# Attention and mixture of experts on one core: matmuls without a reader in the first 28 microseconds

## The chip, the cores and the metric

One core of a Trainium2 chip runs the whole program in one launch. The metric is the device time of that core in microseconds; the time before is 882.89 us, the median of three runs (879.62, 882.89 and 883.45). The core has five engines that each work off a queue of their own in order: TensorE (PE in the profile; PEld are its weight loads), VectorE (DVE), ScalarE (ACT), GpSimd (POOL) and SyncE (SP), which here only starts transfers. [...]

## The reference

Inputs q, k, v have 8 batches, 8 heads, 576 positions and 64 dimensions, in float32. Attention comes first, on rotated q and k:

```
q_rot, k_rot = (rotate(q), rotate(k))
scores = scale * np.matmul(q_rot, k_rot.transpose(0, 1, 3, 2))
attn = softmax(scores)             # over the last axis
x = (attn @ v).transpose(0, 2, 1, 3).reshape(4608, 512)
```

Then each of the 4608 rows of x goes to one of 8 experts, the one with the largest of `x @ w_gate + modality_bias[modality_id]`, and comes out as `gate * (relu(x @ w1[e]) @ w2[e])`, with w1 of 512 x 1024 and w2 of 1024 x 512.

## The kernel before

The attention is worked in 32 pairs of heads (n = 0 to 31), and the experts follow from about 460 us on. A pair passes through these steps, each a Python function that issues instructions:

- `load` brings q and k of the pair, transposed, into a buffer (ST in the profile); `rope_` rotates them in five parts: two products (0 and 1, lines 454 and 456), their sum (2, line 458), a copy that rounds the sum to the matmul's input form (3, by `acopy`, line 445, on ScalarE, into HL), and the remainder of the rounding (4, line 462, also into HL). For pair 0 the vector parts run on VectorE, for pair 1 parts 0 to 2 on VectorE and part 4 on GpSimd, later all on GpSimd.
- `swap` (line 470) copies HL into SW by transfers, with the two halves of 64 partitions exchanged, first the rounded part, then the remainder.
- `scores` (line 485), nine times for a pair (S0 to S8): matmuls of 64 x 128 by 64 x 288, two side by side on the two halves of the rows, one from HL and one from SW, into a slot of two PSUM banks. S0 to S7 take six matmuls each, S8 twelve. There are four slots, ps0 to ps3 (`SL` in the code).
- `rowmin` (line 494, VectorE) takes a slot, writes it to SBUF with the row minimum and frees the slot; `expo` (line 503, ScalarE) takes the exponential.
- `fill` (F0 to F3, FA, FB; `tpose` at line 508) transposes the exponentials on TensorE, 16 instructions of 64 columns in F0 to F3, four in FA, into a slot; `evac` copies the slot out, one bank by ScalarE and one by VectorE (lines 445 and 541).
- `AV` (line 566) multiplies by v; `outp` and `ev` finish the pair.

Pair 0 is rotated in three pieces of columns, `FIRST = ((0, 480), (800, 1152), (480, 800))`, so that the first piece can start early. idf, an identity matrix of 128 x 128, is written by GpSimd at the start.

The order on every engine is fixed by hand. Each step is put into a list of jobs with a time as its key (`KEYS`, and `EDGE` for the first and last pairs, plus 14.438 us for each pair), the list is sorted, and the instructions are issued in that order; PE, ACT, DVE, POOL and SP keep it. For pair 0 TensorE's order is S8, S0, S1, S2, S3, S5, S6, S4, S7, F1, F0, F2, FA, and then the first scores of pair 1, S2, S4, S1, S8, S3, and FB and S0, before the first `AV` of pair 0. `take` chooses a slot when the job is issued, and the framework adds the semaphore waits that the buffers ask for. Pair 0's pieces are rotated by the loop at line 1427, ahead of all these jobs.

Of the kernel before, what the change touches and what calls it, by code (L numbers as in the profile page):

```python
# [53 lines left out]
SLOTS = {  # L54
    "S0": 1, "S1": 2, "S2": 3, "S3": 0, "S4": 2, "S5": 0, "S6": 2, "S7": 0, "S8": 1, "F0": 1, "F1": 3, "F2": 0, "F3": 3, "FA": 2,
    "FB": 2, "AVA": 0, "AVB": 3, "OUT": 1, "RK8": 5, "L1": 0,
}
# [173 lines left out]
def tile_attention_moe(ctx: ExitStack, tc: tile.TileContext, qk, v, mod, wg, mb, w1, w2, rope, cf, ci, out):  # L231
    nc = tc.nc
# [9 lines left out]
    idf = cst.tile([P, P], F32, name="idf")  # L242
# [19 lines left out]
    HL, SW = ([cst.tile([P, 2, TW], F32R, name=f"{nm}{i}") for i in range(2)] for nm in ("HL", "SW"))  # L262
# [45 lines left out]
    SL = [psS.tile([P, 2, 512], F32, name=f"ps{i}") for i in range(4)]  # L308
# [3 lines left out]
    def take(nm, bks, n=None):  # L312

        own = PLACES.get(n, {}).get(nm, SLOTS[nm])
        if nm == "RK8":
            own, bks = own & 3, (own >> 2,)
        if not all((own, b) in idle for b in bks):
            if nm == "RK8":
                own, b = min(idle, key=idle.get)
                bks = (b,)  # L320
            else:
                own = min((i for i in range(4) if all((i, b) in idle for b in bks)), key=lambda i: max(idle[i, b] for b in bks))
        for b in bks:
            del idle[own, b]
        if len(bks) == 2:
            use[own] = []
        return (own, *bks) if nm == "RK8" else own
# [15 lines left out]
    def load(n, half):  # L343
        nc.sync.dma_start(out=Rs[n % 2][:, half], in_=qk[n, :, half])
        st[n] = dict(R=Rs[n % 2], HL=HL[n % 2], SW=SW[n % 2], V=Vs[n % 2])
# [98 lines left out]
    def acopy(o, i, scale=1.0):  # L444
        return nc.scalar.activation(o, i, AF.Copy, scale=scale)  # L445


    def rope_(n, part, c0=0, c1=QW):
        d = st[n]
        e = nc.vector if n == 0 or n == 1 and part < 3 else nc.gpsimd  # L450
        c, o = slice(c0, c1), slice(c0 + 64, c1 + 64)
        a, b = d["R"][:, 0, c], d["R"][:, 1, c]
        if part == 0:
            e.tensor_tensor(a, a, COS[:, c], op=ALU.mult)
        elif part == 1:
            e.tensor_tensor(b, b, SIN[:, c], op=ALU.mult)
        elif part == 2:
            e.tensor_tensor(a, a, b, op=ALU.add)  # L458
        elif part == 3:
            acopy(d["HL"][:, 0, o], a)  # L460
        else:
            e.tensor_tensor(d["HL"][:, 1, o], a, d["HL"][:, 0, o].bitcast(F32), op=ALU.subtract)  # L462

    def swap(n, i, c0=0, c1=QW, eng=nc.sync):
        d = st[n]
        a, b = (d[t].bitcast(F32) for t in ("SW", "HL"))
        for g in range(2):
            c = slice(max(c0 + 64, Q0[0] * g), min(c1 + 64, TW - 64 if g else K1[1]))
            if c.start < c.stop:
                eng.dma_start(out=a[g * 64:g * 64 + 64, i, c], in_=b[64 - g * 64:128 - g * 64, i, c])  # L470
# [35 lines left out]
    def tpose(ps, g, c, src, k0):  # L506
        r = slice(g * 64, g * 64 + 64)
        nc.tensor.transpose(ps[:, g, c:c + 64], src[r, k0:k0 + P], idf[r, r])  # L508

    def fill(n, f):  # L510
        d = st[n]
        own = take(f, (0, 1), n)
        ps = SL[own]
        d[f], d["at", f] = ps, own
        if f[1] in "0123":
            j = int(f[1])
            for i in range(8):
                for g in range(2):
                    tpose(ps, g, i * 64, PJ[j], (S + 64) * (i // 4) + i % 4 * P)
        elif f == "FA":  # L520
            for j in range(2):
                for g in range(2):
                    tpose(ps, g, j * 64, PJ[j], 512)
        else:
            for kt in range(4):
                for g in range(2):
                    tpose(ps, g, kt * 64, P4, 64 + g * 64 + kt * P)
            for g in range(2):
                tpose(ps, g, 256, P4, (1 - g) * S)
            for j in (2, 3):  # L530
                for g in range(2):
                    tpose(ps, g, 192 + j * 64, PJ[j], 512)
# [891 lines left out]
    order.enter_context(tc.manual_schedule(engines=pinned))  # L1424
    dmas = ExitStack()
    dmas.enter_context(tc.manual_schedule(engines={mybir.EngineType.SP}))
    for i, c in enumerate(FIRST):
        for part in range(5):
            rope_(0, part, *c)
            if part > 2:  # L1430
                swap(0, part - 3, *c, eng=(nc.scalar, nc.sync)[part - 3])
        if i == 0:
            load(1, 0)
# [4 lines left out]
    for n in range(NPAIR):  # L1438
# [7 lines left out]
        for f in ("F0", "F1", "F2", "F3", "FA", "FB"):  # L1446
            K_(f, fill, n, f)
            for g in range(2):
                K_(f"{'AB'[g]}_{f}", evac, n, f, g)
        for w in range(2):  # L1450
            c = "AB"[w]
# [243 lines left out]
```

## Time and profile before

| | |
|---|---|
| median of three runs | 882.89 us (879.62 to 883.45) |
| profiled execution, its own time | 888.49 us |
| its span, first to last instruction | 886.6 us, mean granted clock 0.988 |
| PE busy | 838.3 us (95%) |
| DVE busy | 725.3 us (82%) |
| ACT busy | 622.3 us (70%) |
| POOL busy | 649.0 us (73%) |
| chain that ended last, by engine | PE 79%, DVE 7%, issue 5%, ACT 4%, POOL 4%, DMA 1% |

Busy time is an average over the whole span, and says little on the first 30 us. The chain that ended last is followed back from the last instruction, at each step to what released it; "issue" in it is time for which the profile shows no wait. In a timeline a line has the start, the time from first start to last end of a merged group, the engine, the line of the code, the operation, what is written from what, the shape and the number of instructions; in brackets stands the idle time before it and what ended that. Matmuls are pipelined, so the distance from one start to the next tells more than the duration of one.

### The profile page before, as it was taken

Reading aid. Unit: us, or ns where it says so; the run is one execution under the profiler, and the core shown is the slowest. Engines: PE = TensorE matmul, PEld = TensorE weight load, DVE = VectorE, ACT = ScalarE, POOL = GpSimd, SP = SyncE. Lnnn points to the kernel's source line nnn. Section 1 sums busy time; section 2 is a strip of 40 time slices with the busy share of each in tenths; the row PEclk is TensorE's granted clock in tenths of the full one; section 3 lists DMA queues with packets and bytes.
Section 4 is the critical chain, followed back from the end, with each engine's and each line's share of the span. In section 5 each row is a group of like instructions: output and inputs, shape, how many; then the busy total and the mean of one; then the engine's idle time right before and its main releaser. Section 6 shows DMA issues by size and latency. Waiting matters only on the chain.

```text
span 886.6 us, 24920 instructions
## 1 busy us (share of the span) xinstructions
PE 838.3 (95%) x9504; PEld 690.8 (78%) x9504; DVE 725.3 (82%) x1612; ACT 622.3 (70%) x1325; POOL 649.0 (73%) x507
## 2 busy tenths in 40 slices
PE   2899999999999999999989799999999998999995
PEld 2687777777777777777768689898989896989895
DVE  6788888898898988888878788989988986798562
ACT  2897989889898888887964467565646563646453
POOL 3899988988989989999358888886886865334111
PEclk9999999999999999999999999999999998999999
DMA  8766868878788786755847292244445321521330
GB/s 266 222 191 169 265 171 213 175 202 207 193 204 195 201 202 173 223 153 155 228 126 237 86 187 74 78 128 159 159 143 185 109 73 34 167 86 52 113 140 22
DMA packets 84346, 141.06 MB, mean 159 GB/s; under 512 B 27592, under 2 KB 54364, under 8 KB 83192
## 3 DMA queue, kind: packets, MB, share of 16 engines
q1 hardware_dynamic: 73624, 118.28, 49.2%
q0 software_dynamic: 9248, 19.46, 7.0%
q8 instruction: 77, 1.26, 0.6%
q10 hardware_dynamic: 1344, 1.62, 0.6%
q14 instruction: 53, 0.43, 0.2%
HBM read 104.61 MB, written 19.51 MB: 140 GB/s over the span
## 4 chain that ended last, share of the span: by engine, by line
PE 79%; DVE 7%; issue 5%; ACT 4%; POOL 4%; DMA 1%; POOLq 0%; SPq 0%; DVEq 0%; ACTq 0%
PE psY L1326 18%; PE ps L566 16%; PE ps L485 14%; PE psH L1194 12%; PE ps L508 9%; PE ps L601 3%; PE psY L1194 2%; PE ps L1079 1%; PE psH L1079 1%; PE psY L1098 1%; ACT P L503 1%; DVE X L1155 1%; POOL HL L462 1%; DVE W1L L442 1%; DMA SW<-HL 1%
## 5 line engine op out<-in xcount | busy, mean ns | idle before, releaser
L494 DVE CUSTOM_DVE_ANT_1 sc<-ps,ZERO 128x576 f32<-128x576 f32 x288 | 206.6, 749 | 24.8 <-PE ps L485 14.6
L503 ACT ACTIVATE P<-sc,mn 128x576 f32<-128x576 f32 x256 | 196.0, 769 | 5.7 <-DVE mn L494 5.1
L485 PE MATMUL ps<-HL 64*128 64x288 f32 x960 | 170.9, 312 | 14.9 <-ACT HL L445 10.7
L485 PE MATMUL ps<-SW 64*128 64x288 f32 x960 | 170.4, 313 | 5.8 <-DMA SW<-HL 5.6
L485 PEld LDWEIGHTS ps<-HL 64*128 64x128 f32 x960 | 136.5, 191 | 20.7 <-ACT HL L445 10.7
L485 PEld LDWEIGHTS ps<-SW 64*128 64x128 f32 x960 | 136.3, 191 | 10.2 <-issue 7.7
L566 PE MATMUL ps<-PH,AT 128*64 128x320 f32 (+1 forms) x1024 | 139.3, 414 | 2.1 <-DVE PH L541 1.9
L1194 PE MATMUL psH<-HL,W1H 128*128 128x256 f32 x576 | 123.3, 283 | 5.8 <-ACT TB L445 3.0
L1013 POOL DMA_INDIRECT XG<-X,iy x80 | 106.9, 1336 | 29.7 <-issue 20.7
L541 DVE COPY PH<-ps 128x512 f32<-128x512 f32 (+1 forms) x160 | 98.4, 631 | 14.3 <-PE ps L508 8.5
L445 ACT ACTIVATE PH<-ps 128x512 f32<-128x512 f32 (+1 forms) x160 | 85.3, 551 | 33.1 <-PE ps L508 23.1
L566 PEld LDWEIGHTS ps<-PH,AT 128*64 128x64 f32 x1024 | 68.3, 137 | 51.1 <-DVE PH L541 5.3
L1194 PE MATMUL psH<-HL,W1L 128*128 128x256 f32 x384 | 107.9, 281 | 0.0
L462 POOL TENSOR_TENSOR HL<-ST,HL 128x1152 fp32r<-128x1152 f32 x31 | 82.4, 2657 | 34.3 <-ACT HL L445 34.2
L508 PEld LDWEIGHTS ps<-idf,P 64*128 64x128 f32 x2304 | 86.7, 138 | 21.7 <-ACT P L503 9.2
L1326 PE MATMUL psY<-W2H,SW 128*128 128x512 f32 x256 | 102.0, 399 | 1.5 <-issue 1.5
L1013 POOL DMA_INDIRECT AT<-X,iy x68 | 88.2, 1297 | 20.4 <-issue 18.3
L1326 PE MATMUL psY<-W2L,SW 128*128 128x512 f32 x256 | 101.5, 396 | 0.7 <-issue 0.7
L508 PE MATMUL ps<-idf,P 64*128 64x64 f32 x2304 | 98.2, 225 | 3.7 <-ACT AT L445 1.6
L1194 PEld LDWEIGHTS psH<-HL,W1H 128*128 128x128 f32 x576 | 96.1, 190 | 7.1 <-ACT TB L445 3.2
L1109 POOL DMA_INDIRECT out_dram<-sc,ix x36 | 41.8, 1162 | 68.7 <-ACT sc L1108 60.6
L458 POOL TENSOR_TENSOR ST<-ST 128x1152 f32<-128x1152 f32 x30 | 79.6, 2653 | 1.2
(281 smaller groups left out, 1984.7 us busy)
## 6 DMA issues: line engine op xcount, KB each, us to landing
ST<-in_moe_w_dram SPq DMA_DIRECT2D x88, 512.0 KB
ST<-in_qk_dram SPq DMA_DIRECT2D x62, 576.0 KB
SW<-HL SPq DMA_DIRECT2D x124, 216.0 KB
AT<-in_v_dram SPq DMA_DIRECT2D x32, 256.0 KB
X<-X SPq DMA_DIRECT2D x8, 1024.0 KB
XG<-X,iy POOLq DMA_INDIRECT x80
AT<-X,iy POOLq DMA_INDIRECT x68
AT<-in_v_dram SPq DMA_DIRECT2D x64, 16.0 KB
```

The lines of the kernel that those rows point to most:

```text
L445: return nc.scalar.activation(o, i, AF.Copy, scale=scale)
L458: e.tensor_tensor(a, a, b, op=ALU.add)
L462: e.tensor_tensor(d["HL"][:, 1, o], a, d["HL"][:, 0, o].bitcast(F32), op=ALU.subtract)
L485: nc.tensor.matmul(ps[:, g, 0:288], t[:, wq, q0:q0 + P], t[:, wk, k0:k0 + 288], start=(m == 0), stop=(m == len(L) - 1))
L494: nc.vector.tensor_tensor_reduce(sc, d.pop(("S", u))[:, :, 0:288], ZERO.unsqueeze(2).to_broadcast([P, 2, 288]), 1.0, FMAX, ALU.add, ALU.mi ...
L503: nc.scalar.activation(p, sc.rearrange("p a b -> p (a b)"), AF.Exp, bias=mn, scale=-1.0, accum_out=d["sum"][:, u:u + 1])
L508: nc.tensor.transpose(ps[:, g, c:c + 64], src[r, k0:k0 + P], idf[r, r])
L541: alone(d["at", f], g, (nc.vector.tensor_copy if g else acopy)(o, i).ins, int(f[1] in "23B"))
L566: i = nc.tensor.matmul(pa[hh * 64:hh * 64 + 64, 0:c1 - c0], d["V"][:, hh, kt, :], r, start=(kt == 0), stop=(kt == 4))
L1013: inst = nc.gpsimd.indirect_dma_start(out=x[:, t, g, :], out_offset=None, in_=X.rearrange("n (i f) -> (n i) f", f=P)[0:rows], in_offset=ba ...
L1194: nc.tensor.matmul(ps[b][:, r * BLK:r * BLK + BLK], w[:, c, f0:f0 + P], x[:, c, :], start=(first and r == 0 and c == 0 and i == 0), stop=( ...
L1326: nc.tensor.matmul(po[t], hx[:, c, o:o + P], w[:, c, :], start=(k == 0 and c == 2 * q and i == 0), stop=(k == 3 and c == 2 * q + 1 and i = ...
```

## The change

The change adds matmuls whose results nothing reads. It takes nothing away and keeps the order of all other instructions. A helper `turns` issues k matmuls into bank 0 of the slot that S8 of pair 0 will use, before S8 takes it. Fourteen are issued from idf, and then, behind part 3 of the rotation of each of pair 0's three pieces, 9, 14 and 20 from the piece that the copy has just written, with 480, 352 and 320 columns. In `fill`, two matmuls of 480 columns go ahead of the transpositions of F0, F1, F2 and FA of pair 0, into the slot that these transpositions then overwrite.

```
+    def turns(k, w, x):
+        for _ in range(k):
+            nc.tensor.matmul(SL[SLOTS["S8"]][:, 0, 0:x.shape[-1]], w, x, start=True, stop=True)
+
     def fill(n, f):
         d = st[n]
         own = take(f, (0, 1), n)
         ps = SL[own]
+        if n == 0 and f in ("F0", "F1", "F2", "FA"):
+            for _ in range(2):
+                nc.tensor.matmul(ps[:, 0, 0:480], HL[0][:, 0, 64:192], HL[0][:, 0, 64:544], start=True, stop=True)
         d[f], d["at", f] = ps, own
...
+    turns(14, idf, idf)
     for i, c in enumerate(FIRST):
         for part in range(5):
             rope_(0, part, *c)
+            if part == 3:
+                turns((9, 14, 20)[i], HL[0][:, 0, 64:192], HL[0][:, 0, c[0] + 64:c[1] + 64])
             if part > 2:
                 swap(0, part - 3, *c, eng=(nc.scalar, nc.sync)[part - 3])
```

## Rows read from the trace of the kernel before

**Rows 1.** The chain of waits in order of time: start, us, what

```profile
1.67 0.28 POOL idf masks.py:199
...
20.12 2.65 POOL HL L462
...
23.30 6.11 DMA SW<-HL
...
29.46 3.98 PE ps L485 x25
...
34.38 2.38 PE ps L566 x20
```

**Rows 2.** Waits of TensorE, 30 to 60 us: us in total, times, longest

```profile
PE ps L485 <- DMA SW<-HL: 0.4, 1, 0.4
```

**Rows 3.** Timeline of ScalarE, first copies into HL

```profile
7.42 0.60 ACT L445 ACTIVATE HL<-ST 128x480 fp32r<-128x480 f32 x1 [0.70 <-DVE ST L458]
...
10.18 0.50 ACT L445 ACTIVATE HL<-ST 128x352 fp32r<-128x352 f32 x1 [2.16 <-DVE ST L458]
...
12.59 0.47 ACT L445 ACTIVATE HL<-ST 128x320 fp32r<-128x320 f32 x1 [1.92 <-DVE ST L458]
...
18.87 1.17 ACT L445 ACTIVATE HL<-ST 128x1152 fp32r<-128x1152 f32 x1 [5.80 <-DVE ST L458]
```

**Rows 4.** Timeline of VectorE, pair 1's rotation and first row minima

```profile
16.08 1.36 DVE L454 TENSOR_TENSOR ST<-ST,ST 128x1152 f32<-128x1152 f32 x1 [1.22 <-DMA ST<-in_qk_dram]
17.48 1.36 DVE L458 TENSOR_TENSOR ST<-ST 128x1152 f32<-128x1152 f32 x1
19.88 0.76 DVE L494 CUSTOM_DVE_ANT_1 sc<-ps,ZERO 128x576 f32<-128x576 f32 x1 [1.05 <-PE ps L485]
...
21.84 0.76 DVE L494 CUSTOM_DVE_ANT_1 sc<-ps,ZERO 128x576 f32<-128x576 f32 x1 [0.51 <-PE ps L485]
```

**Rows 5.** Timeline of TensorE, 16 to 30 us

```profile
16.58 0.58 PE L485 MATMUL ps<-SW 64*128 64x288 f32 x1 [5.25 <-DMA SW<-HL]
...
18.21 0.44 PE L485 MATMUL ps<-HL 64*128 64x288 f32 x1
...
18.45 0.44 PE L485 MATMUL ps<-HL 64*128 64x288 f32 x1
...
23.57 0.29 PE L485 MATMUL ps<-SW 64*128 64x288 f32 x1
23.70 0.29 PE L485 MATMUL ps<-HL 64*128 64x288 f32 x1
...
25.06 1.29 PE L508 MATMUL ps<-idf,P 64*128 64x64 f32 x32 [0.38 <-ACT P L503]
27.01 0.84 PE L508 MATMUL ps<-idf,P 64*128 64x64 f32 x20 [0.65 <-ACT PH L445]
28.60 0.37 PE L485 MATMUL ps<-HL 64*128 64x288 f32 x1 [0.76 <-ACT AT L445]
```

**Rows 6.** Stretches of TensorE: us, busy (instructions), granted clock, DMA share, GB/s

```profile
29.00:30.00 1.00, 0.64 (x6) 0.65 0.89 336
30.00:31.00 1.00, 1.00 (x12) 0.50 0.20 72
...
32.00:33.00 1.00, 1.00 (x13) 0.65 0.69 221
```

**Rows 7.** Chain of waits, a stretch of matmuls of 256 columns

```profile
465.60 12.15 PE ps L1079 x96
```

**Rows 8.** TensorE, a later gap: its timeline, then a stretch as in rows 6

```profile
448.43 0.37 PE L485 MATMUL ps<-HL 64*128 64x288 f32 x1 [2.09 <-ACT PH L445]
...
449.00:450.00 1.00, 1.00 (x14) 0.57 0.44 91
```

**Rows 9.** Timeline of GpSimd at 356 us

```profile
356.24 2.66 POOL L462 TENSOR_TENSOR HL<-ST,HL 128x1152 fp32r<-128x1152 f32 x1 [0.39 <-ACT HL L445]
```

More of the change, by code (lines that the diff above doesn't have):

```diff
@@ L508, in tpose, with turns @@
         nc.tensor.transpose(ps[:, g, c:c + 64], src[r, k0:k0 + P], idf[r, r])
+    def turns(k, w, x):
+        for _ in range(k):
+            nc.tensor.matmul(SL[SLOTS["S8"]][:, 0, 0:x.shape[-1]], w, x, start=True, stop=True)
     def fill(n, f):
@@ L513, in fill @@
         ps = SL[own]
+        if n == 0 and f in ("F0", "F1", "F2", "FA"):
+            for _ in range(2):
+                nc.tensor.matmul(ps[:, 0, 0:480], HL[0][:, 0, 64:192], HL[0][:, 0, 64:544], start=True, stop=True)
         d[f], d["at", f] = ps, own
@@ L1426, in tile_attention_moe @@
     dmas.enter_context(tc.manual_schedule(engines={mybir.EngineType.SP}))
+    turns(14, idf, idf)
     for i, c in enumerate(FIRST):
@@ L1429, in tile_attention_moe @@
             rope_(0, part, *c)
+            if part == 3:
+                turns((9, 14, 20)[i], HL[0][:, 0, 64:192], HL[0][:, 0, c[0] + 64:c[1] + 64])
             if part > 2:
```

## The prediction

> **What bounds the kernel now.** I read the page's busy shares first (TensorE 95% of the span), then the chain of waits in order of time, because a change to the first 30 us can only count through what that chain holds there. In the chain the reader is to see that TensorE is not on it before 29.46 us [rows 1]: it goes through GpSimd's subtraction for pair 1 (line 462, 20.12 to 22.77), then a transfer SW<-HL of 6.11 us that lands at 29.41, and only then through TensorE's scores of pair 1. From there on TensorE is the chain almost without a break: in the waits of 30 to 60 us it has a single one, 0.4 us, and none in 60 to 90 [rows 2].
>
> What leads to 20.12 contains no TensorE either. ScalarE's copy of pair 1 runs 18.87 to 20.04 [rows 3], after VectorE's sum of 17.48 to 18.84, after VectorE's product at 16.08, which waited for a load of q and k [rows 4]. So 29.41 is set by a load, three vector steps, one ScalarE copy, one GpSimd step and one transfer. Whatever the change gains before 29.41 is gained beside this path. It can pay in one way only: by the speed of TensorE after 29.46.
>
> That speed is the second thing to see [rows 5, 6]. Pairs of score matmuls (one per half of the rows, side by side) follow each other by 0.24 us at 18.21 and 18.45, and by 0.13 us at 23.57 and 23.70. The granted clock is recorded as 1.00 in both stretches, so the record does not show the slow start; the spacing does. [...] Between 25.06 and 29.3 TensorE had done 52 transpositions and a few scores. [...]
>
> **The change part by part.**
>
> *Fourteen matmuls of idf.* idf is written by 1.95 us [rows 1]. Nearest rows: 20 plain f32 matmuls of 256 columns took 2.38 us at full clock, 0.12 each [rows 1], so 0.06 for 128 columns, 0.12 at half clock: 14 x 0.12 = 1.7 us. No row shows a plain f32 matmul of full height and width, so I set the upper end at four times that (6.7 us, to 8.7). The lower end is 14 x 0.06 = 0.8. The next matmuls wait for ScalarE's first copy, done at 8.02 [rows 3]: at the upper end 0.7 us late, otherwise nothing. I take 1.7, by that nearest row.
>
> *Nine, fourteen and twenty matmuls of 480, 352 and 320 columns.* Nearest row: 96 matmuls of 256 columns in 12.15 us, 0.127 each at full clock [rows 7]; by columns that is 0.24, 0.17 and 0.16 us, and twice as much at half clock. They wait for copies that end at 8.02, 10.68 and 13.06 [rows 3]. All at full clock: 8.02 + 2.1 = 10.2; 10.7 + 2.4 = 13.1; 13.1 + 3.2 = 16.3, just ahead of 16.58, when the first scores get their transfer [rows 5]. All at half clock: 8.0 + 4.3 = 12.3, + 4.8 = 17.1, + 6.4 = 23.5, which would make the first scores 6.9 us late. The clock will rise between: in the old kernel it had risen 6 us after the scores began, and 3.2 us after 29.46. A rise at 11.2, after six or seven of the nine, ends the row of matmuls at 11.8 + 2.4 + 3.2 = 17.4; a rise at 14.0, after five of the fourteen, at 15.5 + 3.2 = 18.7. I take 17.9, with 16.6 and 18.7 as ends. Queued behind them on TensorE's in-order queue is everything, but first the scores of pair 0.
>
> *Scores of pair 0 at full clock.* The first row minimum needs 24 score matmuls (S8 has 12, S0 and S1 six each), 12 pairs: 12 x 0.13 = 1.6 us instead of 12 x 0.24 = 2.9. From 17.9 this ends at 19.5 instead of 19.8; VectorE is held by pair 1's sum until 18.84 [rows 4]. After that VectorE sets the pace (0.68 us for a score, three pairs at full clock take 0.4), and its wait of 0.51 us before 21.84 [rows 4] and a smaller one go. So pair 0's exponentials come about 0.3 + 0.7 = 1.0 us earlier (ends 0.2 and 1.7).
>
> *Two matmuls of 480 columns ahead of F1, F0, F2, FA.* Eight in all, 0.24 us each: 1.9 us, 3.8 at half clock. Part lies in TensorE's waits of 0.38 and 0.65 us before the groups [rows 5]. Each pair needs its PSUM slot free, as its group does, so no new wait arises; if the slot comes when the exponentials are ready, they cost their full time. Net: FA, which ended at 27.85, ends between 27.0 (1.7 us earlier, half of the eight hidden) and 28.5 (0.2 earlier, hidden only in those waits). Its cover is the transfer that lands at 29.41: pair 1's first scores start some 0.75 us after FA [rows 5], so about 0.8 us of lateness would still be free. Past that point every microsecond counts in full.
>
> *What is late next.* The same transfer at 29.41. TensorE stands idle before it for about as long as it did, or longer if pair 0 is done sooner: from about 27.8 to 29.46, but for one or two pairs of scores. That is the heart of my forecast. The eight matmuls put some 0.5 us of work in front of each group, but they do not fill this last gap. The trace has a twin of it: TensorE stood idle for 2.09 us to 448.43 in the midst of dense work, ran scores for 0.7 us at full speed, and the granted clock then fell all the same (0.57 from 449 to 450) [rows 8]. I therefore expect the clock to fall near 29 again and the 1.4 us to be lost as before.
>
> Sum on the profiled execution (888.49 us, its span 886.6 and 1.9 around it): 0 before 29.41, 0 after. That run lies 5.6 us above the median 882.89, for reasons that this change does not touch, so the forecast stands at the median: 882.8.
>
> **The rivals.**
>
> *The clock stays up* (faster, by little). For it: what TensorE did before the fall at 29.3 was nearly all transpositions, and the four groups that now get ordinary matmuls are just those. If transpositions do not hold the clock and ordinary matmuls do, the eight stand in the right place. Against it: the gap to 29.46 and its twin. Price: 1.4 us, up to 2.6 if the old kernel's other executions stay slow as long after 29.46 as the start did (6 us, 24 pairs x 0.11). Not all may arrive: GpSimd, which is on the chain from 356.24 with hardly a pause, had waited only 0.39 us there [rows 9], so from 0.4 us on the gain must also have moved GpSimd's earlier work. 0.4 to 2.6 us, 881.5.
>
> [...]
>
> *The added matmuls run at half clock and push pair 0 past the transfer* (slower). Place: TensorE's queue before 29.41. If the clock is not up before about 16 us, and the transposition groups are also at half clock, then the first scores come at 18.7 to 23.5, and eight matmuls cost 3.8 us. It decides at a lateness of 0.8 us of FA. Bounds: 18.7 with all eight in full gives some +1 us after the cover; 23.5 gives 6.9 + 3.8 - 0.8, about +10. For it: nothing has yet run on TensorE at that time, and the rise took 6 us of work in the old kernel. Against it: 43 matmuls without a break are more than 6 us of work. I price it at +3: 886.
>
> *The change doesn't do what it says*: the first scores still run at half clock, because 0.4 to 3 us without work stand between the early groups. Then the added matmuls have only their own time, mostly before 16.58 where TensorE was waiting; pair 0 is 0 to 1 us late, under its cover. Time as before, 883.
>
> **How the numbers follow.** Clock falls again: 0.55, 882.8, own range 880 to 885. Clock stays up: 0.27. Slower: 0.10. Early clock not raised: 0.08. The three runs of before spread over 879.62 to 883.45, and that scatter is as large as any term here. The range must take in 881.5 less the scatter, and the lower part of the slower rival: 878.5 to 886.5. A measurement of this kernel can tell about 0.5%, 4.4 us, from no change. Faster by more than that (below 878.5) needs the full 2.6 us and a lucky scatter, or a stretch that I don't see: 0.17. Slower by more (above 887.3) is the upper part of the slower rival: 0.08. Within: 0.75.
>
> **What would show it.** In the changed profile: score pairs 0.13 us apart from the first on; the first row minimum near 19.5 instead of 19.88; the chain still through GpSimd's line 462 and the SW<-HL transfer landing near 29.4; a granted clock of 0.5 after it. The forecast is wrong if the clock is 1.00 from 29 to 33, or if pair 1's first scores no longer wait for that transfer.

## The result and the profile after

The change makes the kernel slower by 1%: 890.16 us median of six runs (888.09 to 894.11) against 881.23 (879.62 to 883.45), ratio 1.0103, interval 1.008 to 1.0127. Ratios here, and the times of e1, leave disturbed runs out, so a ratio can differ a little from that of the medians beside it. The forecast was 882.8, no change, with a range up to 886.5 and a chance of 0.08 for slower.

The page of the changed kernel: the span, the first line of the busy shares, and the queue that is named "instruction".

```profile
span 888.4 us, 25077 instructions
PE 852.5 (96%) x9583; PEld 703.1 (79%) x9583; DVE 725.7 (82%) x1612; ACT 622.3 (70%) x1325; POOL 648.9 (73%) x507
q8 instruction: 77, 1.26, 0.6%
```

TensorE has 79 matmuls and 79 weight loads more, not 65: each of the 14 plain f32 matmuls counts twice. The two profiled spans differ by 1.8 us only, because the profiled execution of before lost some microseconds between 735 and 747, where TensorE was busy for 8.05 of 12 us and VectorE and ScalarE paused as well; the changed kernel's profile has no such place.

The start, in the chain of waits (start, us, what), is nearly as it was [rows 1]:

```profile
20.25 2.67 POOL HL L462
...
23.45 6.72 DMA SW<-HL
...
30.21 3.46 PE ps L485 x31
```

The same GpSimd step and the same transfer set TensorE's start on pair 1, 0.75 us later than before: the chain had a later load behind it (0.15 us), and the transfer took 6.72 instead of 6.11 us. TensorE's timeline there (start, us, engine, line, operation, count, idle before):

```profile
2.01 5.94 PE L512 MATMUL ps<-idf 128*128 128x128 f32 x28 [2.01 <-POOL idf masks.py:199]
8.41 2.23 PE L512 MATMUL ps<-HL 128*128 128x480 f32 x9 [0.46 <-ACT HL L445]
11.07 5.60 PE L512 MATMUL ps<-HL 128*128 128x352 f32 x34 [0.42 <-ACT HL L445]
16.59 0.40 PE L485 MATMUL ps<-HL 64*128 64x288 f32 x1
...
17.51 0.29 PE L485 MATMUL ps<-HL 64*128 64x288 f32 x1
...
17.65 0.29 PE L485 MATMUL ps<-HL 64*128 64x288 f32 x2
...
27.35 0.71 PE L520 MATMUL ps<-HL 128*128 128x480 f32 x2
27.99 0.34 PE L508 MATMUL ps<-idf,P 64*128 64x64 f32 x4
```

The change does what it says. The added matmuls end just as the first scores get their transfer, the score pairs are 0.13 to 0.14 us apart from 17.4 us on (0.24 before, [rows 5]), and FA ends at 28.33 instead of 27.85. The first row minimum, the line of VectorE that answers to [rows 4], comes a whole microsecond earlier:

```profile
18.88 0.75 DVE L494 CUSTOM_DVE_ANT_1 sc<-ps,ZERO 128x576 f32<-128x576 f32 x1
```

After 30 us the granted clock held, fell and rose again (us, busy, granted clock as a share of full speed, DMA share, GB/s; compare [rows 6]):

```profile
30.00:31.00 1.00, 0.79 (x12) 1.00 0.27 105
31.00:32.00 1.00, 1.00 (x16) 0.65 0.55 72
...
34.00:35.00 1.00, 1.00 (x14) 0.65 0.12 40
```

So at 53 us the changed kernel is 0.7 us behind, and the question is where 8 more come from. VectorE takes one reciprocal for each pair; these are its starts in the kernel before, in us, and how much later it is in the changed kernel:

```
 53 +0.7 | 139 +0.8 | 153 +0.9 | 166 +4.7 | 207 +4.9 | 220 +6.6
248 +6.7 | 261 +7.9 | 275 +8.6 | 357 +8.3 | 435 +9.1 | 480 +9.0
```

Nothing is lost for 100 us, and then it goes in steps, at 160, 217, 258 and 274. TensorE's timeline of the changed kernel at the first three:

```profile
157.95 0.29 PE L485 MATMUL ps<-HL 64*128 64x288 f32 x1
160.13 0.65 PE L508 MATMUL ps<-idf,P 64*128 64x64 f32 x15 [1.89 <-DVE mn L494]
...
216.21 0.40 PE L508 MATMUL ps<-idf,P 64*128 64x64 f32 x6
218.10 0.47 PE L508 MATMUL ps<-idf,P 64*128 64x64 f32 x9 [1.49 <-issue]
...
256.76 0.97 PE L508 MATMUL ps<-idf,P 64*128 64x64 f32 x26
258.91 0.52 PE L508 MATMUL ps<-idf,P 64*128 64x64 f32 x10 [1.18 <-issue]
```

The second and the third stand in the middle of a group of transpositions that all read the same finished data: six of sixteen are done at 216.6, and the next comes 1.49 us later, with "issue" as the reason. No buffer and no semaphore can explain that. At the first, a weight load of the group had already run at 158.52, so the group had begun there too; the releaser that the profile infers is the last thing that ended. The kernel before has no idle time over 0.5 us on TensorE between 60 and 350 us. The first stall also took the clock with it:

```profile
159.00:160.00 1.00, 0.00 (x0) 1.00 1.00 234
...
161.00:162.00 1.00, 1.00 (x13) 0.50 1.03 250
...
164.00:165.00 1.00, 1.00 (x10) 0.79 2.28 92
```

A granted clock of 0.50 from 161.0 to 164.4 is 1.7 us of work lost behind a stall of 1.89: together 3.6 of the 3.8 us of that step.

### The profile page after: what moved, and what is told of

Its sections match the earlier page's. It is cut to its first block, busy times and chain, and to the rows that moved or that the text cites. A ratio compares the mean times of both kernels' runs of the same rounds, so it can differ in the third digit from the quotient of the medians.

```text
span 888.4 us, 25077 instructions
## 1 busy us (share of the span) xinstructions
PE 852.5 (96%) x9583; PEld 703.1 (79%) x9583; DVE 725.7 (82%) x1612; ACT 622.3 (70%) x1325; POOL 648.9 (73%) x507
## 3 DMA queue, kind: packets, MB, share of 16 engines
q8 instruction: 77, 1.26, 0.6%
## 4 chain that ended last, share of the span: by engine, by line
PE 73%; POOL 7%; issue 6%; DVE 5%; ACT 5%; DMA 4%; SPq 0%; POOLq 0%; DVEq 0%; ACTq 0%
PE psY L1333 18%; PE ps L573 13%; PE ps L485 13%; PE psH L1201 12%; PE ps L508 9%; PE ps L608 2%; ACT P L503 2%; PE psY L1201 2%; PE psH L1086 1%; PE psY L1105 1%; POOL HL L462 1%; DMA AT<-X,iy 1%; POOL TAB L734 1%; POOL ST L454 1%; DMA SW<-HL 1%
## 5 line engine op out<-in xcount | busy, mean ns | idle before, releaser
L1020 POOL DMA_INDIRECT AT<-X,iy x68 | 90.0, 1323 | 20.4 <-issue 18.2
```

What stands on the lines that cost most here:

```text
L1020: inst = nc.gpsimd.indirect_dma_start(out=x[:, t, g, :], out_offset=None, in_=X.rearrange("n (i f) -> (n i) f", f=P)[0:rows], in_offset=ba ...
```

## The experiments

**Theory: TensorE runs out of instructions.** The queue "instruction" q8 moves 77 packets, 1.26 MB, 16 KB each. If they are all TensorE's, a packet holds 247 of the 19,008 matmuls and weight loads on average. The experiments take 256 instructions for a whole packet; nothing had shown that number yet, and e2 and e3 try it. In stretches of half a microsecond the packets can be found one by one. In the changed kernel one moves at 144.0, none in the 12 us after it, and the next at 157.0, just before the stall (packets, MB, share of the 16 engines):

```profile
q8 instruction: 1, 0.02, 11.0%
...
q1 hardware_dynamic: 1841, 2.63, 89.6%
...
q8 instruction: 1, 0.02, 15.4%
```

Up to 460 us the median distance is 8 us, and half of them lie between 6 and 9. The stalls at 217 and 258 follow the distances from 202.5 to 215 and from 243 to 256.5; the q1 line is the data that the queues moved from 145 to 157. The change adds 79 x 2 = 158 instructions, so by this theory every later packet boundary stands 158 instructions away from where it stood in the work of a pair. **Rival: the early work itself**, the matmuls ahead of the four groups, the later start of pair 1, the clock.

**e1: the number without the work.** 79 tiny matmuls in TensorE's idle time at the start.

```
+    for _ in range(79):
+        nc.tensor.matmul(SL[SLOTS["S8"]][0:32, 0, 0:32], HL[0][:, 0, 0:32], HL[0][:, 0, 0:32], start=True, stop=True)
     for i, c in enumerate(FIRST):
```

> The kernel before with 79 tiny matmuls (32 rows out, 32 columns, nothing reads them) at the head of TensorE's queue, in the idle time before the first scores: as many TensorE instructions as the change adds (14 plain f32 matmuls count twice in the trace), but no early clock and nothing ahead of the transposition groups. Theory (supply): TensorE's instructions come in packets of 16 KB over the DMA queues, 256 instructions each, and 158 more instructions move every later packet boundary to another place in the work of a pair, where the packet lands late and TensorE stands still in the middle of a transposition group: 888 to 892 us. Rival (early work): the matmuls ahead of F1, F0, F2, FA and the state of pair 0 at 30 us cause the loss; this kernel has none of that: 880 to 883 us.

Measured: 887.8 us median (881.11 to 891.12) against 881.03, ratio 1.0065 (1.0032 to 1.0098). At 153 us its profile is 0.3 us ahead of that of before, at 261 us 6.9 behind; one of its stalls:

```profile
255.53 0.80 PE L508 MATMUL ps<-idf,P 64*128 64x64 f32 x11 [2.57 <-issue]
```

That is just under the theory's range and well over the rival's: a loss comes with the number alone.

**e2 and e3: a whole packet.** e2 keeps what the change does early, but for 38 small matmuls of idf in place of the 14, and brings the number to 256 (the 38 count twice); e3 is e1 with 128 matmuls.

```
-    turns(14, idf, idf)
+    for _ in range(38):
+        nc.tensor.matmul(SL[SLOTS["S8"]][0:32, 0, 0:32], idf[:, 0:32], idf[:, 0:32], start=True, stop=True)
...
-                turns((9, 14, 20)[i], ...
+                turns((9, 14, 21)[i], ...
```

> The changed kernel with 38 small f32 matmuls of 32 columns in place of the 14 of 128, and 21 in place of 20: 128 matmuls, 256 instructions added in all, which is one whole packet. Theory (supply): the boundaries fall where they fell in the kernel before, the stalls at 158, 217 and 258 us go, and the time is that of before within 1.5 us either way: 880 to 883. Rival (early work): everything that the change does early is still there: 888 to 892.

> The kernel before with 128 tiny matmuls at the head of TensorE's queue, 256 instructions, one whole packet. Theory (supply): same boundaries as before, 880 to 883. Rival (any instruction added at the head costs, by number): worse than the run with 79, above 888.

Measured: e2 882.22, ratio 1.001 (0.9988 to 1.0032); e3 879.39, ratio 0.999 (0.9961 to 1.0019). Adding more instructions takes the loss away, as only the theory has it. Both pages list one packet more than before, which is what 256 more instructions of TensorE make if the packets are its own:

```profile
q8 instruction: 78, 1.28, 0.6%
```

In e2's profile the clock held over pair 1's first scores, and at 53 us it was 1.1 us ahead of before.

```profile
30.00:31.00 1.00, 1.00 (x20) 1.00 0.09 28
31.00:32.00 1.00, 0.99 (x15) 1.00 0.81 96
```

It lost these again by stalls of 0.88 us at 170 and 2.27 at 338 (this execution was the slowest of twelve), so the same place of the boundaries is not quite the same luck.

**e4 and e7: one part each.** e4 has only the eight matmuls in `fill`, e7 only those before the first scores.

```
e4  -    turns(14, idf, idf)
    -            if part == 3:
    -                turns((9, 14, 20)[i], ...
e7  -        if n == 0 and f in ("F0", "F1", "F2", "FA"):
    -            for _ in range(2):
    -                nc.tensor.matmul(ps[:, 0, 0:480], ...
```

> Only the eight matmuls of 480 columns ahead of F1, F0, F2 and FA, nothing before the first scores; 16 instructions added. Theory (supply): boundaries moved by a sixteenth of a packet only, near the time of before, 880 to 885. Rival (early work): these eight are the dear part, they push pair 0 past the transfer that pair 1 waits for: 884 to 892, with the loss in the first 35 us.

> The change without the eight matmuls ahead of F1, F0, F2 and FA: only those before the first scores, 71 matmuls as the trace counts them, 142 instructions. Theory (supply): more than half a packet, stalls as in the changed kernel, 886 to 892 us. Rival (the loss is made by the eight): 880 to 883.

Measured: e4 881.09, ratio 0.9996 (0.997 to 1.0022): the eight cost nothing. e7 ran on another chip than e4, where before takes 874.46: 878.82, ratio 1.0049 (1.0026 to 1.0073). That is 4.4 us, where I expected 5 to 11, with stalls of 0.87 at 160 and 1.53 at 215. Its granted clock was also at 0.50 from 29 to 35 us, and at 53 us its profile was 1.1 us behind that of before, so part of the 4.4 may be the clock's.

**e5 and e6: emptier queues.** Both leave out the loads of q and k of pairs 8 to 22, e5 in the kernel before, e6 in the changed one.

```
     def load(n, half):
-        nc.sync.dma_start(out=Rs[n % 2][:, half], in_=qk[n, :, half])
+        if not 8 <= n <= 22:
+            nc.sync.dma_start(out=Rs[n % 2][:, half], in_=qk[n, :, half])
```

> The kernel before without the loads of q and k of pairs 8 to 22 (30 transfers of 576 KB left out; the pairs are worked with what lies in the buffers), so that the DMA queues are less full from about 100 to 300 us. It is the reference for the next run: TensorE had no stall over 0.5 us between 60 and 350 us, so it should gain little, 876 to 882 us.

> The changed kernel without the same 30 loads. Theory (supply over crowded DMA queues): the packets of TensorE's instructions no longer land late in that stretch, the stalls at 158, 217 and 258 us go, and the kernel comes within 3 us of the run of before without these loads. Rival (the stalls come from the place of the packet boundary alone, whatever the queues carry, for instance a fixed cost of a packet change): the three stalls stay, 1.2 to 1.9 us each, and the distance stays at 7 to 10 us.

Measured in one comparison: e5 872.91, ratio 0.9975 (0.996 to 0.999); e6 873.23, ratio 0.999 (0.9976 to 1.0005). The changed kernel's distance is 0.3 us instead of 6 to 9. All waits of its TensorE from 60 to 350 us are (us in total, times, longest):

```profile
PE ps L486 <- DVE AT L549: 0.8, 4, 0.2
```

and in the changed kernel with its loads, over the same stretch:

```profile
PE ps L508 <- issue: 2.9, 3, 1.5
PE ps L508 <- DVE mn L494: 1.9, 1, 1.9
PE ps L573 <- DVE PH L548: 1.2, 4, 0.6
PE ps L485 <- DVE AT L548: 0.8, 4, 0.2
```

Between 100 and 285 us the longest distance between two packets is 9.0 us in e6, and 13.5 in the changed kernel. So in these runs it took both, the boundary at that place and crowded queues.

**e8, e11, e12: a row of numbers; e9 and e10.** e8, e11 and e12 are e1 with 32, 64 and 96; e9 is the changed kernel again; e10 is e4 with 24 tiny matmuls at the head.

> The kernel before with 32 tiny matmuls at the head of TensorE's queue, 64 instructions, a quarter of a packet. Theory (supply): the time follows the place of the boundary, between no shift (881) and 158 instructions (888 to 893); which way a quarter goes the theory can't say, 877 to 890, but stalls with no semaphore behind them must be found in its trace if it is over 884 and not if it is under 880. Rival (more added instructions, more time): 882 to 886.

> The changed kernel once more, unaltered, so that the next three have it on their own chip. Theory (supply): slower than before again, by 7 to 10 us, with stalls of TensorE inside transposition groups. Rival (the loss belongs to one chip): within 2 us of before.

> The version that the runs point to: the eight matmuls ahead of F1, F0, F2 and FA, which kept the granted clock at 1.00 over the first scores of pair 1, and 24 tiny matmuls at the head of the queue, so that 64 instructions are added, a quarter of a packet, where 32 tiny matmuls alone were not slower. Theory (supply, and the clock held): 1 to 3 us under before. Rival (the clock's share is too small to see, or the packets fall differently): within 1 us of before, or above.

> 64 tiny matmuls at the head, 128 instructions, half a packet. Theory (supply): near the place of the kernel with only the early matmuls (142 instructions, 4 us over before), so 2 to 9 us over before. Rival (only the change's own number is bad, the rest is flat): within 1.5 us of before.

> 96 tiny matmuls at the head, 192 instructions, three quarters of a packet. Theory (supply): the time must come back to that of before as the number goes on to 256, so between the run with 158 instructions and that of before: 0 to 8 us over it. Rival (time grows with the number added): more over before than the run with 64 by half or more.

All of them, by the number of instructions added (before took 881.03 us beside e1 to e4, 874.46 beside e5 to e8 and 874.57 beside e9 to e12, on three chips):

```
added  kernel          ratio    interval
   16  e4              0.9996   0.997  to 1.0022
   64  e8              0.9985   0.9972 to 0.9999   (873.41 us against 874.46)
   64  e10             0.9982   0.9967 to 0.9997   (872.63 us against 874.57)
  128  e11             1.0024   1.0008 to 1.004    (876.72 us)
  142  e7              1.0049   1.0026 to 1.0073
  158  the change      1.0103   1.008  to 1.0127
  158  the change, e9  1.0063   1.0041 to 1.0085   (880.41 us)
  158  e1              1.0065   1.0032 to 1.0098
  192  e12             1.0074   1.0048 to 1.01     (881.09 us)
  256  e3              0.999    0.9961 to 1.0019
  256  e2              1.001    0.9988 to 1.0032
```

The time rises to 0.6 to 1.0% between 158 and 192 and is back at a whole packet. Up to 192 the times alone would also fit a rise with the number, and e12 met the condition of that rival (6.5 us over before, e11 2.2); the return at 256 rules it out. e11 came out at the low end of what I expected, e9 under it (5.8 us, where I had 7 to 10). The ranges for e5 and e8 were set by a before of 881 us; both times fall under them on their chip, and inside them if the 6.8 us that before is faster there are added. The profiles of e8, e10 and e11 have no stall over 0.5 us on TensorE from 60 to 350 us; that of e11 is its fastest execution, 873.51, so where its other runs lost their 2 us isn't shown. e12's stalls, again without a semaphore:

```profile
213.44 0.39 PE L485 MATMUL ps<-SW 64*128 64x288 f32 x1 [2.99 <-issue]
271.08 0.29 PE L485 MATMUL ps<-HL 64*128 64x288 f32 x1 [1.77 <-issue]
```

**Where the stalls stand among the instructions.** The traces hold a sharper sign. These are the matmuls (first and third line) and the weight loads that had started in the changed kernel when the stalls at 160 and 218 us ended (in brackets):

```profile
0.00:160.12 160.12, 152.75 (x2239) 0.99 0.75 212
0.00:160.12 160.12, 119.06 (x2240) 0.99 0.75 212
0.00:218.09 218.09, 208.60 (x3123) 0.98 0.77 204
0.00:218.09 218.09, 161.21 (x3124) 0.98 0.77 204
```

So 4,479 and 6,247 together, and 7,510 at the third stall. For the other stalls over 0.5 us between 60 and 350 us that have no semaphore behind them, the same count gives 4,479, 6,247 and 8,015 in e9; 4,478, 7,509 and 9,782 in e1; 4,478 and 6,246 in e7; 6,247, 8,015 and 9,782 in e12; 4,986, 6,754, 8,522 and 10,290 in e2; 8,265 in e4. The steps are whole multiples of about 252.6, although the work at these numbers differs from kernel to kernel: 1,768 from the first stall to the second is seven steps. And each time TensorE goes on 1.2 to 1.8 us after a packet of q8 has landed, the 17th at 4,479, the 24th at 6,247, the 31st at 8,015: seven packets for seven steps. So what TensorE waits for is the next packet. That a step is 252.6 and not 256 would be so if three or four instructions of each packet are of kinds that the count leaves out; that isn't shown.

e10 is the version that beats both, by 1.9 us over before and by some 8 over the change. It can't be told from e8, which has none of the change's matmuls, so how much of it is the clock and how much the packets stays open.

## Why the prediction was wrong

**The step that failed** is the sentence that whatever the change gains can pay in one way only, by TensorE's speed after 29.46 us, and with it the sum "0 before 29.41, 0 after". Every added instruction was priced by the time it takes in TensorE's queue, and that time was indeed covered. Its other effect had no term: it moves all later instructions of that engine against the packets they come in. The runs put 6 to 9 us in its place for 158 instructions (waits for packets, and the clock that fell behind some), and e1 shows the loss without any of the priced work.

**The slower rival** had another mechanism, and it did not happen: no added matmul ran past the transfer.

**The terms.** Idf's matmuls took 5.94 us, near my upper end of 6.7 and not 1.7: each counts twice, and most of the 28 took 0.21 us, where I had 0.12 for each of 14. The row that I took the price from was misread: its 20 matmuls are ten of the code (`AV` of the first half), already counted twice, and they run in pairs that start together (0.01 us apart, the next pair 0.22 later). The first copy of pair 0 covered the error. The nine, fourteen and twenty ended at about 16.6, my early end; the starts of idf's matmuls go from 0.21 to 0.11 us apart at 7.4 us, so the rise came there and not between 11 and 14 (by the spacing alone: the granted clock is given as 1.00 from 2 us on). The first row minimum came at 18.88, where I had 19.5. FA ended at 28.33, inside 27.0 to 28.5. The transfer stayed the gate, as forecast.

**The clock.** I gave 0.55 to a fall near 29 us. In the changed kernel's first profile the clock fell at 31.3 us, after a wait of 1.24 us for the late transfer; but in e9, the same kernel, and in the four other profiles with the eight matmuls (e2, e4, e6, e10) it stayed at 1.00 until 38 us. Of the eight without them it fell in six (before, e1, e3, e5, e7, e12) and stayed in two (e8, e11). The rival "the clock stays up" was the better reading, though one profile each is thin, and several chips are mixed. The 1.4 us of the forecast was an estimate from [rows 5, 6], some 13 pairs from 29.46 to 32.7 at 0.24 - 0.13 = 0.11 us each; no run shows it as such, and it was rather high: at 53 us the seven profiles in which the clock stayed up are 0.6 us ahead of before on average (from 1.1 ahead to 0.2 behind), the six others in which it fell 0.1 behind (from 0.7 ahead to 1.1 behind), so some 0.7 us, half of the 1.4. So the clock stayed up in five of six profiles with the eight and in two of eight without, against what I read from the twin gap [rows 8]; whether the transpositions or the short waits beside them let it fall, no run separates. What decided the result was not the clock at 30 us.

**The reading that I missed.** The page of before lists q8 with 77 packets, 1.26 MB, and I took it for a detail. How many packets TensorE can hold ahead, no run here shows; few is my estimate, since by the count above a packet lands 5 to 6 us (median) before the first of its instructions in most profiles, less than the median distance of 8 us, and 13 us without a packet were enough to stop the engine in the changed kernel (144.0 to 157.0).

**What stays open.** A long distance between packets does not make a stall by itself: the profile of before has one of 13.0 us (from 68 to 81) and one of 12.5 (from 209.5 to 222) without any. Carried over to before, the count of instructions says why: these two packets landed about 2.4 and 1.5 us ahead of their first instruction, just in time. In e6, with the emptier queues, that lead is never under 3 us between 100 and 285 us. When a packet is asked for, and whether and where it waits behind data, these views don't show. Nor is it known why the change lost 1.0% in its first runs and 0.6% in e9, on a chip where before takes 874.57; in the profiles the first stall cost 3.8 us with the fall of the clock, and 1.6 in e9, where the clock stayed up. And "issue" alone proves nothing: in before TensorE has five such waits between 736 and 743 us, up to 1.51 us, amid a DMA share of 0.14, with pauses of over 3 us on VectorE and ScalarE; no run says what they are, nor what the 2.08 us at 457.7 in the changed kernel are, 4 us after the last packet.

## What to carry to other kernels

Instructions that looked free at the head of a full queue were not free here: 158 of them cost 6 to 9 us, since they moved every later boundary between the packets that TensorE's instructions come in, and 0.3 us where 30 loads of data were left out of the queues (e6). So when a small edit gives a loss that starts a hundred microseconds after it, look for idle time labelled "issue" in the middle of a group with one set of inputs, and for a packet of instructions that landed just before it ended (1.2 to 1.8 us here), and repeat the run with the number of added instructions brought to a whole packet (256 here) before judging the edit. Half a per cent lost can be the place of the boundaries and not the idea. Whether as much can be won by it isn't shown: the most that tiny matmuls alone won is 0.15%, in e8.

## What the hardware showed that was not expected

A stall of instructions cost more than its length where the granted clock fell to 0.50 behind it: the 1.89 us at 160 became 3.8, against 1.6 in e9, where the clock stayed at 1.00. A plain f32 matmul of 128 columns is two matmuls with two weight loads in the trace, 0.21 us each until 7.4 us and 0.11 after. And the stalls stood at fixed places in TensorE's stream of instructions, 252.6 matmuls and weight loads apart or whole multiples of that (1,768 from 4,479 to 6,247), and not at fixed places in the work.
